# Attention into GELU MLP on one core: how batch 0's masks, transposes and weighing are laid out

## The chip, the cores and the metric

The kernel runs on one core of one Trainium2 chip. The metric is the device time of one launch in microseconds (us), lower is better. The kernel before took 353.18 us (median of 5 runs, 352.17 to 354.53).

## The reference

Eight batches of eight heads, sequence 576, head dimension 64. Each head is causal attention with a forgetting decay; the heads are then joined to tokens of width 512, and the tokens go through a two-layer MLP with exact GELU (width 2048 inside).

```
scores = q @ k.T / sqrt(D)
cum    = cumsum(log(clip(f, 0.0001, 1)))
scores = where(j > i, -1e9, scores + cum[i] - cum[j])
attn   = softmax(scores);  o = attn @ v
x      = o as [B*S, H*D];  h = x @ w_in;  out = gelu(h) @ w_out
```

Inputs and output are float32; the kernel multiplies in bfloat16 and accumulates in float32.

## The kernel before, in words

**Layout.** Heads go in four pairs i = 0 to 3; a pair's q and k lie transposed in `qT[i]`, `kT[i]` as [128, 576], head 0 of the pair on partitions 0 to 63 and head 1 on 64 to 127. Scores are computed transposed (keys on partitions), so the two heads' matmuls of one block contract over 64 rows each, in the two halves of TensorE's array ("64-row tiles"). The causal 576 x 576 square is cut into five key blocks, and these are packed into four score tiles t = 0 to 3 of 448, 448, 448 and 320 columns for each head (`STILES`); tile 0 holds two diagonal blocks, the others one each (`SDIAG`). One score tile takes two PSUM banks (one for each head); the pool `s_psum` has two such tiles, `o_psum` and `m_psum` have two banks each.

**A score tile** (`scores`, L289 to L314): TensorE fills it, ScalarE takes the exponential of all of it into `e` (L314), and the tile is free for the next but one. For batch 0, and for pair 0 of batch 1, the causal mask is added by TensorE ahead of the scores: for each diagonal block and head a 128-row matmul of an identity with `after`, a 128 x 128 tile of 0 and -1e9 (L295), and then the scores on top (L304), cut after the first 128 columns. For all other pairs GpSimd zeroes the masked part of `e` (L316).

**Decay.** The factor exp(-cum[j]) is multiplied into v (and stands beside it as a 65th column) by GpSimd in `weigh_v` (L279, L285), which needs v in `v_sb` and the factors in `wT`; what belongs to the query cancels in the softmax. `attend` (L335) multiplies e with the weighed v for each head into one `o_psum` bank; `normalize` divides by the 65th column on VectorE (L350, L351) and hands the tail of 64 rows on (L361 on VectorE, or L359 on ScalarE for pair 2). `to_xT` transposes the result for the MLP (L373).

**The order of batch 0 is written out by hand** in `first_attention`: warm-up matmuls, the transposes of each pair's k and q (`transposes_first`, L192, copied out by VectorE at L199; pair 0's q by ScalarE), score tiles, the transposition of the factors (L528), `attend_head` for the eight heads between the last two pairs' score tiles, and the first four blocks of the MLP's first product (`gemm1`, L398, GELU at L411). Engines run their own instructions in this order. GpSimd's queue holds, besides, every load of q, k, w_in and w_out (issued by it, and cast on the way): before the attention the masks and the loads of batch 0, and inside it `weigh_v(0, i)`, the quarters of w_in, and q and k of batch 1. SyncE's queue loads v; batch 1's v waits for the memset of `v_sb` that stands behind `weigh_v(0, 3)` on GpSimd.

**After the attention of batch 0** come gemm1 blocks 4 to 15 (`ffb`). Among them stand the transposes of batch 1's pairs 0 to 2 (`transposes_pe`, L220, eight VectorE copies each at L232), after blocks 6, 8 and 13; after block 9 GpSimd is given `weigh_v(1, 0)`, the other quarters of w_out, q and k of batch 2 and `weigh_v(1, 1)`. The transposes of pairs 0 and 1 use `s_psum`, those of pair 2 both banks of `o_psum`. `second_attention` then runs batch 1's scores with the second product of batch 0 (`gemm2`, L438) in the gaps, and transposes pair 3, again into both banks of `o_psum`, after score tile (0, 2). Batches 2 to 7 run in `attention`, with the second product of the batch before in their gaps (L487); the tails of all batches make a last MLP pass.

Of the kernel before, what the change touches and what calls it, by code (L numbers as in the profile page):

```python
# [50 lines left out]
def kernel(  # L51
# [57 lines left out]
    def load_v(b, h0=0, h1=H):  # L109
# [9 lines left out]
    f_sb = consts.tile([BH, S], FP32)  # L119
    nc.sync.dma_start(f_sb, f.rearrange("b h s -> (b h) s"))  # L120
    load_qk_tokens(0, 0, 2)
    ident_bf = consts.tile([P, P], BF16)
    make_identity(nc, ident_bf)
    load_qk_tokens(0, 2, 4)
    load_qk_tokens(0, 4, 6)
    after = consts.tile([P, P], BF16)
    nc.gpsimd.memset(after, 0.0)
    nc.gpsimd.affine_select(
        out=after,
        in_=after,  # L130
        compare_op=Alu.is_ge,
        fill=-1.0e9,
        base=0,
        pattern=[[1, P]],
        channel_multiplier=-1,
    )
    nc.gpsimd.memset(v_sb[:, :, 0, 0:1], 0.0)
    load_v(0, 0, 4)
    load_qk_tokens(0, 6, 8)
# [149 lines left out]
    def scores(b, i, t):  # L289
        on_pe = b == 0 or (b == 1 and i == 0)  # L290
        st = s_psum.tile([P, 2, 512], FP32, tag="s", name=f"s{t}")

        for x, c in enumerate(SDIAG[t] if on_pe else []):
            for h in range(2):
                nc.tensor.matmul(  # L295
                    st[:, h, c : c + P], ident_bf, after, start=x == 0, stop=False
                )
        c, width = 0, sum(w for _, _, w in STILES[t])
        for n, q0, w in STILES[t]:
            cut = P if on_pe and c in SDIAG[t] and w > P else w  # L300
            for a0, a1 in ((0, cut), (cut, w)):
                for h in range(2 if a1 > a0 else 0):
                    d = slice(h * D, (h + 1) * D)
                    nc.tensor.matmul(  # L304
                        st[:, h, c + a0 : c + a1],
                        kT[i][d, K0[n] : K0[n] + P],
                        qT[i][d, q0 + a0 : q0 + a1],
                        start=not on_pe,
                        stop=not on_pe or c + a1 == width,
                    )  # L310
            c += w
        et = e_pool.tile([P, 2, 512], BF16, tag=f"e{t}", name=f"e{t}")
        e_of[b, i, t] = et
        nc.scalar.activation(et[:, :, 0:c], st[:, :, 0:c], Act.Exp, scale=scale)  # L314
        for c0 in [] if on_pe else SDIAG[t]:
            nc.gpsimd.affine_select(  # L316
                out=et[:, :, c0 : c0 + P],
                in_=et[:, :, c0 : c0 + P],
                compare_op=Alu.is_ge,
                fill=0.0,  # L320
                base=0,
                pattern=[[0, 2], [1, P]],
                channel_multiplier=-1,
            )
# [184 lines left out]
    def first_attention():  # L509


        def transposes(i, pool, tag):
            transposes_first(i, 1, pool, tag)
            transposes_first(i, 0, pool, tag)

        def attend_head(i, h):
            attend(0, i, h, (0, 1, 2, 3, 4))
            return normalize(0, i, h)

        warm_up(9)  # L520
        transposes(0, o_psum, "o")
        warm_up(4)
        scores(0, 0, 0)
        transposes(1, m_psum, "m")
        scores(0, 0, 1)
        psw = o_psum.tile([P, NBLK, BH], FP32, tag="o", name="psw")
        for n in range(NBLK):
            nc.tensor.transpose(  # L528
                psw[:, n, :], wk[:, K0[n] : K0[n] + P], ident_fp[:BH, :BH]
            )  # L530
        nc.vector.tensor_copy(wT[:, 0:4, :], psw[:, 0:4, :])
        nc.vector.tensor_copy(wT[D:P, 4, :], psw[D:P, 4, :])
        scores(0, 0, 2)
        scores(0, 0, 3)
        transposes(2, m_psum, "m")
        scores(0, 1, 0)
        scores(0, 1, 1)
        scores(0, 1, 2)
        transposes(3, m_psum, "m")
        scores(0, 1, 3)  # L540
        weigh_v(0, 0)
        load_w_in(0)
        load_w_in(1)
        weigh_v(0, 1)
        load_qk_tokens(1, 0, 4)
        weigh_v(0, 2)
        weigh_v(0, 3)
        load_w_in(2)
        load_w_in(3)
        nc.gpsimd.memset(v_sb[:, :, 0, 0:1], 0.0)  # L550
        load_v(1, 0, 4)
        load_v(1, 4, 8)
        load_qk_tokens(1, 4, 8)
        scores(0, 2, 0)
        attend_head(0, 0)
        scores(0, 2, 1)
        attend_head(0, 1)
        scores(0, 2, 2)
        scores(0, 2, 3)
        attend_head(1, 0)  # L560
        scores(0, 3, 0)
        attend_head(1, 1)
        to_xT(0, 0, nc.vector.tensor_copy)
        scores(0, 3, 1)
        scores(0, 3, 2)
        attend_head(2, 0)
        scores(0, 3, 3)
        attend_head(2, 1)
        to_xT(0, 1, nc.scalar.copy)
        last = [attend_head(3, 0)]  # L570
        both = s_psum.tile([P, 2, 1024], BF16, tag="s", name="ps_x2")
        to_xT(0, 2, nc.scalar.copy, ps=both[:, 0, 0:TC])
        last.append(attend_head(3, 1))

        pss = [gemm1(0, ffb, (0, 1)) for ffb in range(2)]
        to_xT(0, 3, nc.vector.tensor_copy, ps=both[:, 1, 0:TC])
        for tail, r in last:
            nc.vector.tensor_scalar(*tail, r[D:P, 4:5], None, Alu.mult)
        more = s_psum.tile([P, 2, 512], FP32, tag="s", name="ps1")
        pss += [more[:, 0, :], more[:, 1, :]]  # L580
# [88 lines left out]
    for b in range(B):  # L669
# [9 lines left out]
        for ffb in range(0 if b else 4, n_ff):  # L679
            gemm1(b, ffb)  # L680
            if b == 0:
                if ffb in (6, 8, 13):
                    transposes_pe(
                        1, (6, 8, 13).index(ffb), s_psum if ffb < 10 else o_psum
                    )
                if ffb == 9:
                    weigh_v(1, 0)
                    for c in range(1, 4):
                        load_w_out(c)
                    load_qk_tokens(2)  # L690
# [42 lines left out]
```

The softmax here doesn't subtract the row's maximum and nothing guards it: scores larger than these inputs give would overflow.

## Time and profile before

| what | value |
|---|---|
| median of 5 runs | 353.18 us (352.17 to 354.53) |
| the profiled execution | 352.18 us; its span 349.8 us, so 2.4 us lie around the span |
| granted TensorE clock | 0.998 |
| busy: TensorE, ScalarE, VectorE, GpSimd | 338.9, 215.2, 203.6, 124.5 us (97, 62, 58, 36%) |
| warm-up and first transposes (batch 0) | 1.25 to 8.9 us |
| attention of batch 0, up to its first gemm1 matmul | 8.9 to 26.7 us |
| gemm1 of batch 0 | 26.7 to 43.6 us |
| attention of batch 1 with gemm2 of batch 0 | 43.6 to 70.6 us |

Times inside the span are counted from its start. A line of the timeline gives the start, the busy time, the engine, the line of the kernel, the operation with what it writes and reads, the number of instructions merged into it, and in brackets how long the engine was idle before and which engine released it. A line of the chain of waits gives start, length and the work that the end of the program hangs on, merged. TensorE's matmuls are pipelined: the chain shows how long a group holds up what follows, and the timeline's busy time overlaps its neighbours.

### The profile page before, as it was taken

To read this page: it belongs to the slowest core of one execution; us is meant where nothing else is said; L and a number is where in the kernel's file an instruction comes from. 1 tells how busy PE (TensorE), PEld (TensorE's weight loads), DVE (VectorE), ACT (ScalarE), POOL (GpSimd) and SP (SyncE) were. 2 spreads that over 40 slices of the span, in tenths; PEclk is the share of its full clock that TensorE was granted. 3 is DMA by queue.
4 is the path that set the end of the run, shared out by engine and by line. 5 is a ranking of instruction groups with operands and counts; after the bars stand their busy time and mean duration, and the time that the engine had idled before them with its cause. 6 is when DMAs were issued, how large, how long until landed. Compare 5 with 4: busy or idle time off the path is not lost.

```text
span 349.8 us, 7804 instructions
## 1 busy us (share of the span) xinstructions
PE 338.9 (97%) x3122; PEld 176.1 (50%) x3122; DVE 203.6 (58%) x501; ACT 215.2 (62%) x296; POOL 124.5 (36%) x243
## 2 busy tenths in 40 slices
PE   8998989999999999999999999999999999999995
PEld 3674544544555455545554455445544554444443
DVE  4562984596469936894579557956696563011011
ACT  5796586457874787468746874687567774603600
POOL 7390185405538044713453245514450530000000
PEclk9999999999999999999999999999999999999999
DMA  7999999986994999298928893679710131011013
GB/s 109 179 185 188 202 140 177 189 190 134 195 179 127 133 208 155 83 137 165 197 77 123 120 214 104 106 134 209 126 39 0 47 89 41 2 60 60 2 31 89
DMA packets 101219, 43.24 MB, mean 124 GB/s; under 512 B 80000, under 2 KB 96640, under 8 KB 101184
## 3 DMA queue, kind: packets, MB, share of 16 engines
q1 hardware_dynamic: 83888, 28.60, 41.3%
q0 software_dynamic: 16896, 13.63, 26.4%
q8 instruction: 24, 0.39, 0.5%
q10 hardware_dynamic: 400, 0.52, 0.4%
q14 instruction: 11, 0.09, 0.1%
HBM read 36.85 MB, written 9.44 MB: 132 GB/s over the span
## 4 chain that ended last, share of the span: by engine, by line
PE 87%; ACT 9%; issue 2%; DMA 1%; DVE 0%; POOL 0%; ACTq 0%; POOLq 0%
PE ps L398 36%; PE ps L487 18%; PE ps L438 12%; PE o L335 10%; PE s L304 8%; ACT e L314 5%; ACT L314 2%; ACT g L411 2%; PE ps_f L192 1%; PE s L295 1%; DMA k<-in_k_dram 1%; PE ps_x L373 1%; PE ps_w L181 1%; PE ps_t L220 0%; PE s_t L220 0%
## 5 line engine op out<-in xcount | busy, mean ns | idle before, releaser
L411 ACT ACTIVATE g<-ps 128x512 bf16<-128x512 f32 x144 | 85.8, 597 | 83.3 <-PE ps L398 83.3
L314 ACT ACTIVATE e<-s 128x896 bf16<-128x896 f32 (+1 forms) x128 | 103.8, 862 | 30.9 <-PE s L304 30.4
L398 PE MATMUL ps<-xT,w_in_sb 128*128 128x512 bf16 x512 | 112.6, 379 | 1.0 <-ACT g L411 1.0
L487 PE MATMUL ps<-w_out_sb,g 64*128 64x512 bf16 (+1 forms) x690 | 102.3, 376 | 0.0
L316 POOL TENSOR_SCALAR_AFFINE_SELECT e<-e 128x256 bf16<-128x256 bf16 x135 | 53.5, 406 | 113.6 <-ACT e L314 112.4
L398 PEld LDWEIGHTS <-w_in_sb 128*128 128x128 bf16 x576 | 56.0, 98 | 67.9 <-issue 3.0
L279 POOL TENSOR_TENSOR vw<-v_sb,wT 128x640 bf16<-128x640 f32 x32 | 41.1, 1285 | 47.1 <-PE ps L398 15.9
L487 PEld LDWEIGHTS <-g 64*128 64x128 bf16 (+1 forms) x690 | 37.6, 94 | 25.5 <-issue 1.6
L304 PE MATMUL s<-qT,kT 64*128 64x320 bf16 (+5 forms) x424 | 46.8, 272 | 2.5 <-ACT e L314 2.0
L263 DVE COPY qT<-tq 64x288 bf16<-64x288 bf16 x96 | 45.1, 470 | 1.5
L335 PEld LDWEIGHTS <-e 128*128 128x128 bf16 x960 | 35.7, 98 | 17.9 <-issue 11.1
L438 PE MATMUL ps<-w_out_sb,g 128*128 128x512 bf16 (+2 forms) x208 | 44.3, 363 | 0.0
L335 PE MATMUL o<-vw,e 128*128 128x65 bf16 x960 | 41.9, 194 | 0.4 <-ACT e L314 0.4
L495 DVE COPY ot<-ps 128x512 f32<-128x512 f32 x24 | 16.5, 689 | 36.0 <-PE ps L487 36.0
L447 DVE COPY ot<-ps 128x512 f32<-128x512 f32 (+2 forms) x13 | 8.4, 650 | 48.9 <-PE ps L438 48.7
L263 DVE COPY kT<-tk 64x288 bf16<-64x288 bf16 x96 | 32.3, 336 | 1.6
L304 PEld LDWEIGHTS <-kT 64*128 64x128 bf16 x424 | 20.0, 94 | 25.9 <-issue 13.2
L350 DVE RECIPROCAL r<-o 128x5 f32<-128x5 f32 x64 | 12.5, 195 | 29.2 <-PE o L335 28.2
L351 DVE TENSOR_TENSOR x<-o,r 128x256 bf16<-128x256 f32 x64 | 27.2, 425 | 2.2
L438 PEld LDWEIGHTS <-g 128*128 128x128 bf16 x208 | 18.7, 98 | 19.1 <-issue 0.6
L361 DVE TENSOR_SCALAR xt<-o,r 64x64 bf16<-64x64 f32 x60 | 17.4, 290 | 1.4
L497 DVE TENSOR_TENSOR ot<-ot,ps 128x512 f32<-128x512 f32 x24 | 16.5, 687 | 1.3
(61 smaller groups left out, 147.2 us busy)
## 6 DMA issues: line engine op xcount, KB each, us to landing
out_dram<-ot SPq DMA_DIRECT2D x32, 256.0 KB, 2.2
v_sb<-in_v_dram SPq DMA_DIRECT2D x20, 256.0 KB, 4.7
v_sb<-in_v_dram SPq DMA_DIRECT2D x29, 128.0 KB, 5.8
q<-in_q_dram POOLq DMA_DIRECT2D x6, 576.0 KB, 6.5
k<-in_k_dram POOLq DMA_DIRECT2D x6, 576.0 KB, 8.5
w_in_sb<-in_moe_w_in_dram POOLq DMA_DIRECT2D x4, 512.0 KB, 8.2
w_out_sb<-in_moe_w_out_dram POOLq DMA_DIRECT2D x4, 512.0 KB, 8.8
q<-in_q_dram POOLq DMA_DIRECT2D x4, 144.0 KB, 4.6
```

The lines of the kernel that those rows point to most:

```text
L263: nc.vector.tensor_copy(rows[:, odd], src[odd * D : (odd + 1) * D, 2 * i + h].rearrange("d j p -> d p j"),)
L279: nc.gpsimd.tensor_tensor(vw_of[b][:, hs, :, 0:D], v_sb[:, hs, :, :], w.unsqueeze(3).to_broadcast([P, 2, NBLK, D]), Alu.mult,)
L304: nc.tensor.matmul(st[:, h, c + a0 : c + a1], kT[i][d, K0[n] : K0[n] + P], qT[i][d, q0 + a0 : q0 + a1], start=not on_pe, stop=not on_pe or ...
L314: nc.scalar.activation(et[:, :, 0:c], st[:, :, 0:c], Act.Exp, scale=scale)
L316: nc.gpsimd.affine_select(out=et[:, :, c0 : c0 + P], in_=et[:, :, c0 : c0 + P], compare_op=Alu.is_ge, fill=0.0, base=0, pattern=[[0, 2], [ ...
L335: nc.tensor.matmul(o[:, m, :], e_of[b, i, t][:, h, c : c + P], vw_of[b][:, 2 * i + h, n, :], start=(n == 0), stop=(n == m),)
L351: nc.vector.tensor_tensor(x_of[b, i][:, :, h, :], o[:, 0:4, 0:D], r[:, 0:4].unsqueeze(2).to_broadcast([P, NBLK - 1, D]), Alu.mult,)
L361: nc.vector.tensor_scalar(*tail, r[D:P, 4:5], None, Alu.mult)
L398: nc.tensor.matmul(ps, w_in_sb[:, kt, ffb * P : (ffb + 1) * P], src[:, kt, :], start=(kt == 0), stop=(kt == n_dm - 1),)
L411: nc.scalar.activation(g_of[c][ffb], ps, Act.Gelu)
L438: nc.tensor.matmul(pss[ts][:, c0:c1], g_of[c][kt][:, ts * P : (ts + 1) * P], w_out_sb[:, kt, c0:c1], start=(kt == 0), stop=(kt == n_ff - 1),)
L487: nc.tensor.matmul(banks[r], g_of[c][kt][rows, ts * P : (ts + 1) * P], w_out_sb[rows, kt, :], start=(kt == 0), stop=last if r else kt == n ...
```

## The change

- **Masks.** In place of the 128 x 128 `after`, two tiles of [128, 2, 128] are built, `key_of` (ones where partition p is column p + 64·half, an identity in two halves of 64 rows) and `after` (the mask's rows in the same two halves). GpSimd builds both on partitions 0 to 63, and VectorE copies them to 64 to 127. A masked block is now one score matmul over the block's whole width for each head, then two mask matmuls of 64 rows for each head, 64 and 128 columns wide, each head's in the half of the array in which its scores are. This holds wherever TensorE masks: batch 0 and pair 0 of batch 1.
- **Order of batch 0's score tiles.** The transposes of pairs 1 and 2 come one score tile later than before, and later score tiles come ahead of the attends: (0,0) and (0,1) now precede the transposes of pair 1, (1,0) those of pair 2; (0,3) follows the factors' transposition before they are copied out; (2,1) and (2,2) come before head (0,0), (2,3) before (0,1), and so on to (3,3) before head (2,0).
- **GpSimd's queue.** The loads of q and k for pair 1 go ahead of the identity. `weigh_v(0, 0)` to `(0, 3)` stand together, with w_in quarters 0 and 1 after the first two, then the memset of `v_sb` and the loads of batch 1's v; the first half of batch 1's q and k, which stood between `weigh_v(0, 1)` and `(0, 2)`, follows after that, and then w_in quarters 2 and 3.
- **Transposes of batch 1** stand after gemm1 blocks 7, 9 and 15 in place of 6, 8 and 13.

```diff
+    load_qk_tokens(0, 2, 4)
     ident_bf = consts.tile([P, P], BF16)
     make_identity(nc, ident_bf)
-    load_qk_tokens(0, 2, 4)
     load_qk_tokens(0, 4, 6)
-    after = consts.tile([P, P], BF16)
-    nc.gpsimd.memset(after, 0.0)
-    nc.gpsimd.affine_select(
-        out=after,
...
+    key_of = consts.tile([P, 2, P], BF16)
+    after = consts.tile([P, 2, P], BF16)
+    for t, op, fill in (
+        (key_of, Alu.not_equal, 1.0), (after, Alu.is_ge, -1.0e9)
+    ):
+        nc.gpsimd.memset(t[0:D], 0.0)
+        nc.gpsimd.affine_select(
+            out=t[0:D],
+            in_=t[0:D],
+            compare_op=op,
+            fill=fill,
+            base=0,
+            pattern=[[-D, 2], [1, P]],
+            channel_multiplier=-1,
+        )
...
-        for x, c in enumerate(SDIAG[t] if on_pe else []):
-            for h in range(2):
-                nc.tensor.matmul(
-                    st[:, h, c : c + P], ident_bf, after, start=x == 0, stop=False
-                )
-        c, width = 0, sum(w for _, _, w in STILES[t])
+        c = 0
         for n, q0, w in STILES[t]:
-            cut = P if on_pe and c in SDIAG[t] and w > P else w
-            for a0, a1 in ((0, cut), (cut, w)):
-                for h in range(2 if a1 > a0 else 0):
+            masked = on_pe and c in SDIAG[t]
+            for half in range(-1, 2 if masked else 0):
+                for h in range(2):
                     d = slice(h * D, (h + 1) * D)
+                    if half < 0:
+                        to = st[:, h, c : c + w]
+                        ab = kT[i][d, K0[n] : K0[n] + P], qT[i][d, q0 : q0 + w]
+                    else:
+                        last = (half + 1) * D
+                        to = st[:, h, c : c + last]
+                        ab = key_of[d, half, :], after[d, half, 0:last]
                     nc.tensor.matmul(
-                        st[:, h, c + a0 : c + a1],
-                        kT[i][d, K0[n] : K0[n] + P],
-                        qT[i][d, q0 + a0 : q0 + a1],
-                        start=not on_pe,
-                        stop=not on_pe or c + a1 == width,
+                        to, *ab, start=half < 0, stop=half == 1 or not masked
                     )
...
         warm_up(9)
         transposes(0, o_psum, "o")
+        nc.vector.tensor_copy(key_of[D:P], key_of[0:D])
+        nc.vector.tensor_copy(after[D:P], after[0:D])
         warm_up(4)
         scores(0, 0, 0)
+        scores(0, 0, 1)
         transposes(1, m_psum, "m")
-        scores(0, 0, 1)
+        scores(0, 0, 2)
         psw = o_psum.tile([P, NBLK, BH], FP32, tag="o", name="psw")
...
+        scores(0, 0, 3)
         nc.vector.tensor_copy(wT[:, 0:4, :], psw[:, 0:4, :])
         nc.vector.tensor_copy(wT[D:P, 4, :], psw[D:P, 4, :])
-        scores(0, 0, 2)
-        scores(0, 0, 3)
+        scores(0, 1, 0)
         transposes(2, m_psum, "m")
-        scores(0, 1, 0)
         scores(0, 1, 1)
         scores(0, 1, 2)
         transposes(3, m_psum, "m")
         scores(0, 1, 3)
-        weigh_v(0, 0)
-        load_w_in(0)
-        load_w_in(1)
-        weigh_v(0, 1)
-        load_qk_tokens(1, 0, 4)
-        weigh_v(0, 2)
-        weigh_v(0, 3)
-        load_w_in(2)
-        load_w_in(3)
+        for i in range(HP):
+            weigh_v(0, i)
+            if i < 2:
+                load_w_in(i)
         nc.gpsimd.memset(v_sb[:, :, 0, 0:1], 0.0)
         load_v(1, 0, 4)
         load_v(1, 4, 8)
+        load_qk_tokens(1, 0, 4)
+        load_w_in(2)
+        load_w_in(3)
         load_qk_tokens(1, 4, 8)
         scores(0, 2, 0)
+        scores(0, 2, 1)
+        scores(0, 2, 2)
         attend_head(0, 0)
-        scores(0, 2, 1)
+        scores(0, 2, 3)
         attend_head(0, 1)
-        scores(0, 2, 2)
-        scores(0, 2, 3)
+        scores(0, 3, 0)
         attend_head(1, 0)
-        scores(0, 3, 0)
+        scores(0, 3, 1)
         attend_head(1, 1)
+        scores(0, 3, 2)
         to_xT(0, 0, nc.vector.tensor_copy)
-        scores(0, 3, 1)
-        scores(0, 3, 2)
+        scores(0, 3, 3)
         attend_head(2, 0)
-        scores(0, 3, 3)
         attend_head(2, 1)
...
-                if ffb in (6, 8, 13):
+                if ffb in (7, 9, 15):
                     transposes_pe(
-                        1, (6, 8, 13).index(ffb), s_psum if ffb < 10 else o_psum
+                        1, (7, 9, 15).index(ffb), s_psum if ffb < 10 else o_psum
                     )
```

More of the change, by code (lines that the diff above doesn't have):

```diff
@@ L121 @@
     load_qk_tokens(0, 0, 2)
+    load_qk_tokens(0, 2, 4)
     ident_bf = consts.tile([P, P], BF16)
     make_identity(nc, ident_bf)
-    load_qk_tokens(0, 2, 4)
     load_qk_tokens(0, 4, 6)
-    after = consts.tile([P, P], BF16)
-    nc.gpsimd.memset(after, 0.0)
-    nc.gpsimd.affine_select(
-        out=after,
[L130 to L135, printed above, removed]
-    )
+    key_of = consts.tile([P, 2, P], BF16)
[13 more added lines that the diff above has]
+        )
     nc.gpsimd.memset(v_sb[:, :, 0, 0:1], 0.0)
@@ L291, in scores @@
         st = s_psum.tile([P, 2, 512], FP32, tag="s", name=f"s{t}")
-        for x, c in enumerate(SDIAG[t] if on_pe else []):
-            for h in range(2):
-                nc.tensor.matmul(
-                    st[:, h, c : c + P], ident_bf, after, start=x == 0, stop=False
-                )
-        c, width = 0, sum(w for _, _, w in STILES[t])
+        c = 0
         for n, q0, w in STILES[t]:
-            cut = P if on_pe and c in SDIAG[t] and w > P else w
-            for a0, a1 in ((0, cut), (cut, w)):
-                for h in range(2 if a1 > a0 else 0):
+            masked = on_pe and c in SDIAG[t]
+            for half in range(-1, 2 if masked else 0):
+                for h in range(2):
                     d = slice(h * D, (h + 1) * D)
-                    nc.tensor.matmul(
-                        st[:, h, c + a0 : c + a1],
-                        kT[i][d, K0[n] : K0[n] + P],
-                        qT[i][d, q0 + a0 : q0 + a1],
-                        start=not on_pe,
-                        stop=not on_pe or c + a1 == width,
+                    if half < 0:
[5 more added lines that the diff above has]
+                        ab = key_of[d, half, :], after[d, half, 0:last]
+                    nc.tensor.matmul(
+                        to, *ab, start=half < 0, stop=half == 1 or not masked
                     )
```

## The prediction

> **What bounds the kernel now.** I read the page first (TensorE 97% busy, clock 0.998), then the chain of waits, then ScalarE's timeline in batch 0's attention, because all that the change touches lies before 50 us. There the chain changes between TensorE and ScalarE:
>
> ```profile
> 10.79 0.22 PE s L295 x2
> 11.00 0.32 PE s L304 x4
> 11.32 0.02 issue
> 11.34 0.93 ACT e L314
> ...
> 16.74 0.25 PE s L304 x4
> 16.99 0.33 PE s L295 x4
> 17.32 0.30 PE s L304 x8
> 17.62 0.58 PE o L335 x15
> 18.20 0.11 PE s L295 x2
> 18.31 0.30 PE s L304 x4
> ```
>
> The sizes of a switch are in these lines. At 2.4 columns per ns two masks are 256 columns, 0.11; the x4 of L304 stream 448 columns for each head, both heads at once, 0.19. Between attends they take 0.11 + 0.30: 0.11 is lost going into 64-row tiles and out again. Between two masked tiles (16.99) the masks take 0.33 for 0.21: another 0.11 going back to 128 rows.
>
> ```profile
> 11.34 2.34 ACT L314 ACTIVATE e<-s 128x896 bf16<-128x896 f32 x3 [0.60 <-PE s L304]
> 14.24 2.53 ACT L314 ACTIVATE e<-s 128x896 bf16<-128x896 f32 x3 [0.56 <-PE s L304]
> 17.03 4.12 ACT L314 ACTIVATE e<-s 128x640 bf16<-128x640 f32 x5 [0.25 <-PE s L304]
> 21.34 0.92 ACT L314 ACTIVATE e<-s 128x896 bf16<-128x896 f32 x1 [0.18 <-PE s L304]
> 22.55 1.73 ACT L314 ACTIVATE e<-s 128x896 bf16<-128x896 f32 x2 [0.29 <-PE s L304]
> 24.39 0.31 ACT L359 ACTIVATE xt<-o,r 64x64 bf16<-64x64 f32 x1
> 24.72 0.70 ACT L314 ACTIVATE e<-s 128x640 bf16<-128x640 f32 x1
> ```
>
> ScalarE starves for TensorE five times in these lines, 1.9 us in all. Where it doesn't (11.34 to 12.17, 14.24 to 15.06) exponentials of 896 start 0.82 apart, one of 640 is passed in 0.63. Sixteen need 12 x 0.82 + 4 x 0.63 = 12.4 us, and take 9.83 to 25.42. The last is late since an `xt` stands before it in the queue.
>
> Later, at the seam of batches 0 and 1, VectorE and ScalarE matter:
>
> ```profile
> 44.21 1.28 ACT L314 ACT_TABLE_LOAD   x1
> 44.72 1.95 DVE L232 COPY kT<-ps_t 64x288 bf16<-64x288 bf16 x4
> 46.47 0.27 PE L295 MATMUL s<-after,ident_bf 128*128 128x128 bf16 x2 [0.90 <-ACT e L314]
> 47.44 1.95 DVE L232 COPY qT<-ps_t 64x288 bf16<-64x288 bf16 x4 [0.77 <-PE ps_t L220]
> ```
>
> VectorE copies batch 1's transposes back to back, 3.96 us for each pair (34.80, 38.76, 42.72), and is done 0.77 before it gets pair 3's. DMA is nearly full:
>
> ```profile
> 20.00:30.00 10.00, 9.22 (x152) 6.16 (x149) 5.84 (x19) 8.47 (x14) 6.83 (x11) 1.00 1.25 197
> 30.00:40.00 10.00, 9.37 (x63) 4.83 (x63) 5.05 (x11) 5.73 (x11) 0.00 (x0) 1.00 1.24 193
> ```
>
> The last two columns are the DMA share and GB/s: the engines are full from 18 to 43 us.
>
> **What the Trainium skill says.** "TensorE: Matmul & The Clock Gate", "The mechanism": matmuls in different row groups run at once; the 0.30 of the x4 above agrees (one after another would be 0.37 without a switch). The same page, "Back-to-back issue gap", puts a floor of about 25 ns under a small matmul: that is my upper price for a pair of 64-wide masks, 2 x 25 = 50 ns; the lower is their 64 columns, 27 ns; no such pair is in the trace as a mask. "ScalarE: Activation LUTs", "What ACT_TABLE_LOAD costs": back-to-back activations overlap by some 93 ns; here 0.92 long and 0.82 apart. "DMA: Bandwidth & Descriptors", "Issuing engines are not separate DMA queues": v from SyncE and weights from GpSimd share the same engines, as the full DMA rows above let one expect.
>
> **The change, part by part.**
>
> *Masks.* Before, a pair has five blocks x 2 x 128 columns = 0.53 us of masks. After: five x (64 + 128) columns, both heads at once, 0.40; with 50 ns for the narrow pair 0.52. A tile's columns become 832, 640, 640, 512, that is 0.35, 0.27, 0.27, 0.21 us, plus 0.11 where a 128-row group is the neighbour. Gain 0 to 0.13 for each pair; I take 0.1. Masks also stop switching: where score tiles follow one another nothing is lost.
>
> *Building the masks.* Two memsets and two selects over 256 columns instead of one each over 128. A 128-wide memset and select take 0.30 and 0.24 from start to next start (5.96, 6.26, 6.50); with twice the columns some 0.42 and 0.36, so 1.56 for 0.54: the memset of v, batch 0's v loads and pair 3's q, k are issued 1.0 later. Pair 3's q, k land at 12.9 behind a full queue and are needed after 14. v paces `weigh_v(0,0)`, at 14.70; its loads took 5.4 to 6.1 us in a full queue, so part of the 1.0 is absorbed: I take 0.3, bounds 0 and 1.0. Its reader, head (0,0), comes at 17.4 against 16.5: hidden, and still with 0.9. The identity, behind two loads more (0.65 each), is ready at 4.8; the first transposes wait for k until 5.67. VectorE's two copies (some 0.2 each) run at 7.4 to 7.8; masks are first wanted at 9. All nothing, covered by the loads and the warm-up.
>
> *Order.* I went through TensorE's and ScalarE's queues with these durations: an exponential starts when ScalarE is free (0.82 or 0.63) and its tile is filled; a tile is filled when TensorE gets there and the exponential two before has ended (start + 0.92 or 0.70, + 0.04). Transposes 0.74, attend 0.58. Up to 10.2 us TensorE streams at half rate (warm-up matmuls 0.43 apart), so tile (0,0) ends at 9.7.
>
> ```
> exponential of   (0,1)  (1,0)  (1,1)  (1,3)  (2,0)  (2,3)  (3,0)  (3,1)  (3,3)
> before           11.34  14.24  15.06  17.03  17.66  20.46  21.34  22.55  24.72
> after, worked    10.54  12.82  13.93  15.57  16.20  18.66  19.40  20.40  22.20
> ```
>
> 0.8 comes from (0,1) ahead of pair 1's transposes, 0.6 more from (1,0) ahead of pair 2's. Pair 3's q transposes then wait 0.2 for VectorE's copy of pair 2's q (`m_psum`), under an exponential. (3,3) no longer stands behind an `xt`. Head (3,0), which got its last input at 25.48, runs at 23.2 to 23.8; head (3,1) ends at 24.65. The chain's first L398 began at 26.67: 2.0 earlier. What is late next is each small refill by TensorE (0.1 to 0.2 at (3,0), (3,1), (3,2)), counted.
>
> *GpSimd's queue.* `weigh_v` ends at 16.5, 18.5, 20.7, 22.0 (1.28 + 0.22, and 0.79 for each load between); heads want them at 17.4, 19.3, 21.8, 23.2: the smallest gap 0.8. The DMA order stays the same. q, k of batch 1 are issued 3.2 later, at 22.2, but the quarter of w_in ahead of them lands only at 25.3 + 0.3. Batch 1's v is issued 2.5 earlier and takes its share (0.045 of 0.2 MB per us after 28 us) earlier, so what stands behind lands some 0.6 later, less once v is done. w_in's third quarter landed at 31.1 and would at 31.9; block 8 wants it at 33.6. The fourth: 35.3 for 37.6. Pair 2's k: 39.3 for 40.7. w_out's first: 42.0 before, 42.9 after, wanted at 41.8: 1.1 of waiting, under the pause for the table load and the exponential (next score at 44.0) and the next point. All hidden.
>
> *Transposes after blocks 7, 9, 15.* The third set (0.51) no longer stands ahead of block 14's GELU, so the last GELU, the table load and batch 1's first exponential come 0.5 earlier still. But VectorE starts 0.86 later (four matmuls of 0.215) and its chain of copies ends 0.86 later against TensorE: pair 3's k transposes, which need pair 2's second bank, wait until 45.55 and end at 45.8, instead of 47.66 with no wait. So of 2.0 + 0.5, 1.85 arrives there; the pair 0 masks of batch 1 behind give 0.05.
>
> *Sum.* 1.9 us. From 50 us on TensorE is 100% busy in the windows and all its weights come earlier, so the gain should stay. Profiled 352.18 - 1.9 = 350.3; the median of runs stands 1.0 above that execution, so 353.18 - 1.9 = 351.3.
>
> **Rivals.**
> - *The refill holds it.* If each of the twelve large tiles waits out the end of the one before (0.93 apart, as in the chain, not 0.82), 12 x 0.11 = 1.3 is lost, of which the refills already counted (0.4) are part: gain 1.0, 352.2. For: `s_psum` has two tiles only. Against: 0.82 is seen where TensorE was ahead.
> - *Given back to DMA.* The seam pays for w_out or block 8 for w_in: about 1 us, 352.4. For: full DMA rows. Against: gaps of 1.3 to 2.3 us by my landings.
> - *Slower.* One place: block 8 waiting for w_in's third quarter, if the q, k loads issued at 22.2 leave the queue empty, or v's earlier stream takes half of it. Each us of landing past 33.6 costs one; past 35.5 (31.1 before) the kernel is slower; at 36.6 it gives 354.3. For: issue leads the queue's end by only 3.4 us. Against: w_in's first quarter, issued at 16.06, moved at the full rate from 18.
> - *Seam without the wait.* If VectorE's copies hold nothing, 2.5 arrive: 350.7.
> - That the masks are no cheaper costs 0.4 and belongs to the forecast's spread.
>
> **Chances.** Forecast 0.59 (own range 350.6 to 352.0), refill 0.13, DMA 0.12, slower 0.10, no wait 0.06. The range reaches from 350.3 to 353.3. 0.5% (1.8 us) is about what a measurement can tell from no change; the forecast lies just past it, so I give two thirds of its chance to faster: with the last case 0.47; same 0.43, slower 0.10.
>
> **What would show it.** Right: ScalarE's pauses between the first and last exponential of batch 0 under 0.8 us in all (1.9 in the lines above); the first gemm1 matmul near 24.6; no mask group of 128 rows; a wait of TensorE's pair 3 transposes for VectorE near 45; score tile (0,3) of batch 1 near 47. Wrong: exponentials 0.9 apart, a wait at gemm1 block 8 or at the first gemm2 matmuls longer than the pause there, or `weigh_v(0,0)` after 16.

## The result, and the profile after

| | before | after |
|---|---|---|
| median | 352.89 us (351.50 to 356.71, 80 runs) | 355.41 us (351.84 to 358.73, 43 runs) |
| ratio to before | | 1.0041, 95% interval 1.0025 to 1.0056 |
| the profiled execution, span, granted clock | 352.18, 349.8, 0.998 | 356.37, 354.1, 0.990 |

The change makes the kernel slower: 0.4% by the ratio, 2.5 us by the medians. The ratio leaves out executions over 1.5% above the fastest of the same kernel (7 of the 44 of after), the medians keep them. Forecast were 351.3 us and a range of 350.3 to 353.3, so both the size and the sign are wrong.

The chain of waits on the page of after, in shares of the span:

```profile
PE 76%; DMA 8%; ACT 7%; POOL 3%; SPq 3%; issue 1%; DVE 0%; POOLq 0%; ACTq 0%
PE ps L401 31%; PE ps L490 18%; PE ps L441 12%; PE o L338 8%; PE s L311 6%; ACT e L317 4%; DMA w_out_sb<-in_moe_w_out_dram 4%; DMA v_sb<-in_v_dram 4%; SPq L114 3%; ACT L317 2%; POOL vw L285 1%; ACT g L414 1%; PE ps_x L376 1%; POOL q L102 1%; POOL k L102 1%
```

Before, TensorE had 87% of it and DMA 1%. Now w_out has 4%, and v with the queue that issues it 7%: that is the first thing to see, ahead of any timeline.

**The attention of batch 0 did get faster.** ScalarE's timeline of the kernel after, where `e` are exponentials and `g` GELUs:

```profile
8.22 4.08 ACT L317 ACTIVATE e<-s 128x896 bf16<-128x896 f32 x5 [0.84 <-PE s L311]
12.51 1.73 ACT L317 ACTIVATE e<-s 128x896 bf16<-128x896 f32 x2 [0.21 <-PE s L311]
14.60 3.73 ACT L317 ACTIVATE e<-s 128x640 bf16<-128x640 f32 x5 [0.36 <-PE s L311]
18.65 0.92 ACT L317 ACTIVATE e<-s 128x896 bf16<-128x896 f32 x1 [0.32 <-PE s L311]
19.87 2.47 ACT L317 ACTIVATE e<-s 128x896 bf16<-128x896 f32 x3 [0.30 <-PE s L311]
...
26.85 1.57 ACT L414 ACTIVATE g<-ps 128x512 bf16<-128x512 f32 x3 [0.78 <-PE ps L401]
...
42.29 1.28 ACT L317 ACT_TABLE_LOAD   x1 [0.43 <-PE s L311]
```

Before, the first GELU stands here:

```profile
29.01 1.57 ACT L411 ACTIVATE g<-ps 128x512 bf16<-128x512 f32 x3 [0.84 <-PE ps L398]
```

ScalarE's waits for scores between the first and the last exponential sum to 1.2 us (1.9 before), and the first GELU starts at 26.85 for 29.01. So 2.16 us are gained in this pair of executions, and at the table load of the seam (ScalarE fetches the table of exponentials again) 1.9 are still there (42.29 for 44.21).

**They are lost twice, both times to w_out.** TensorE's timeline of the kernel after (scores are L311, gemm2 L441):

```profile
42.23 0.25 PE L311 MATMUL s<-after,key_of 64*128 64x64 bf16 x4
44.52 1.04 PE L441 MATMUL ps<-w_out_sb,g 128*128 128x512 bf16 x4 [2.04 <-ACT e L317]
...
48.60 0.37 PE L311 MATMUL s<-qT,kT 64*128 64x320 bf16 x4 [0.67 <-ACT e L317]
...
48.91 0.36 PE L338 MATMUL o<-vw,e 128*128 128x65 bf16 x6
52.47 1.01 PE L441 MATMUL ps<-w_out_sb,g 128*128 128x512 bf16 x2 [3.20 <-DMA w_out_sb<-in_moe_w_out_dram]
53.41 0.56 PE L311 MATMUL s<-qT,kT 64*128 64x448 bf16 x2
...
54.39 1.47 PE L441 MATMUL ps<-w_out_sb,g 128*128 128x512 bf16 x3
```

The same places before:

```profile
44.53 1.04 PE L438 MATMUL ps<-w_out_sb,g 128*128 128x512 bf16 x4
...
49.73 0.37 PE L304 MATMUL s<-qT,kT 64*128 64x320 bf16 x4 [0.66 <-ACT e L314]
...
50.23 0.59 PE L438 MATMUL ps<-w_out_sb,g 128*128 128x512 bf16 x2
```

The first wait of after is put down to `e`, but gemm2 doesn't read `e`: it reads g and w_out, and w_out's first quarter, issued at 26.66, landed 17.8 later, at 44.5. Before, the same group started at 44.53 without a wait, so the lead is used up at this point; it comes back in part (the scores behind `e` start at 48.60 for 49.73), since the score tiles ahead of it were early. The second wait is plain: 3.20 us for w_out's second quarter. Before, that group began at 50.23 without one.

Then the clock. The same kernel by stretches (columns: busy time and instructions of TensorE, its weight loads, VectorE, ScalarE, GpSimd; then granted clock, DMA share, GB/s):

```profile
20.00:30.00 10.00, 8.53 (x121) 5.29 (x118) 5.07 (x17) 7.31 (x12) 7.35 (x12) 1.00 1.23 198
30.00:40.00 10.00, 9.84 (x66) 4.97 (x65) 6.28 (x14) 5.98 (x11) 3.17 (x5) 1.00 1.24 194
...
48.00:50.00 2.00, 0.66 (x10) 0.38 (x10) 1.93 (x5) 2.00 (x3) 0.56 (x2) 1.00 1.21 109
50.00:52.00 2.00, 0.00 (x0) 0.00 (x0) 0.27 (x1) 0.17 (x1) 0.69 (x2) 0.61 0.91 107
52.00:54.00 2.00, 1.53 (x6) 0.31 (x6) 0.00 (x0) 0.00 (x0) 1.29 (x3) 0.50 1.27 202
54.00:56.00 2.00, 2.00 (x14) 0.78 (x14) 0.91 (x3) 0.92 (x1) 0.95 (x2) 0.50 1.29 206
56.00:58.00 2.00, 2.00 (x24) 1.17 (x22) 0.72 (x3) 0.70 (x1) 1.28 (x3) 0.69 1.31 203
```

From 20 to 40 DMA is as full as before. TensorE stood still from 49.3 to 52.5; its clock falls to half at 50.4, in the middle of this wait, and stays there until 57.2: three matmuls of L441 take 1.47 above, 0.81 at full clock (e1 at 52.39). The books of the two profiled executions, by how much after is ahead (-) or behind (+): -2.16 at the first GELU, -1.13 behind w_out's first quarter, +2.24 at the second, +4.3 when batch 1's attention is over, and +4.3 at the end (354.1 for 349.8). So in this pair of executions 1.0 goes to the first quarter, 3.4 to the second and 2.1, the rest, to the clock.

**Why w_out is late.** The DMA rows in slices of half a microsecond from 36 to 56, first of before, then of after:

```profile
DMA  9999999999996976500669999999999999999999
GB/s 192 196 195 195 193 198 203 195 217 270 267 230 126 225 180 132 82 9 0 53 37 162 207 180 205 186 156 201 211 199 176 182 137 160 203 186 216 200 201 201
...
w_out_sb<-in_moe_w_out_dram POOLq DMA_DIRECT2D x3, 512.0 KB, 7.6
...
tails<-xt SPq DMA_TRANSPOSE x1, 3.1
```

```profile
GB/s 193 192 192 197 188 190 192 193 203 188 196 198 196 193 206 196 219 188 194 190 193 171 157 137 116 112 107 101 69 34 123 201 204 199 198 205 210 203 201 211
...
w_out_sb<-in_moe_w_out_dram POOLq DMA_DIRECT2D x3, 512.0 KB, 15.6
...
tails<-xt SPq DMA_TRANSPOSE x1, 16.2
```

What GpSimd and SyncE issued, first of before, then of after:

```profile
42.51 1.99 SPq L385 DMA_TRANSPOSE tails<-xt  x1
...
42.78 1.28 POOL L279 TENSOR_TENSOR vw<-v_sb,wT 128x640 bf16<-128x640 f32 x1 [15.94 <-PE ps L398]
...
44.14 2.31 POOL L159 DMA_DIRECT2D w_out_sb<-in_moe_w_out_dram  x3
```

```profile
36.83 1.28 POOL L285 TENSOR_TENSOR vw<-v_sb,wT 128x640 bf16<-128x640 f32 x1 [9.38 <-DMA v_sb<-in_v_dram]
...
36.89 5.58 SPq L388 DMA_TRANSPOSE tails<-xt  x1
...
38.20 2.31 POOL L165 DMA_DIRECT2D w_out_sb<-in_moe_w_out_dram  x3
```

Before, the queues run dry at 45, and the tails' DMA transpose (`x_tail_dma`, SyncE, issued at 42.5) lands in 3.1 us. After, there is no lull: GpSimd got batch 1's v at 36.83 rather than 42.78, so three quarters of w_out and batch 2's q, k are issued 6 us earlier. The transpose, issued at 36.9, lands 16.2 later, and from 46.5 the rate sinks step by step to 34 GB/s, until 51. The packet records of after show what sinks (q0 is GpSimd's queue, q1 SyncE's; start of the half microsecond from the span's start, packets started in it, kB, median and longest packet in ns):

```
 45.50 q0 n=  74 kB=  75.8 med=  96 max=  129 | q1 n=  77 kB=  19.2 max=   82
 46.00 q0 n=  80 kB=  76.8 med=  96 max= 4761 | q1 n=  78 kB=  19.7 max=   31
 47.00 q0 n=  65 kB=  62.5 med=  96 max= 3719 | q1 n=  66 kB=  15.9 max= 3729
 50.00 q0 n=  28 kB=  26.6 med=  96 max= 1116 | q1 n=  32 kB=   7.9 max= 1202
 51.50 q0 n=  85 kB=  86.0 med=  96 max=  153 | q1 n=  81 kB=  14.7 max=  102
```

Single packets of both queues last 4.8, 3.7, 1.2 us, the later they start the shorter: 27 of them start between 46.4 and 50.8, and all end at 51.2 to 51.3. It looks as if each DMA engine that comes to its part of the transpose stands still, with both queues, until the last one comes to it. That picture is inferred; that the transpose is what does it is tested below.

### The profile page after: what moved, and what is told of

It is laid out like the page before. It is cut to its first block, busy times and chain, and to the rows that moved or that the text cites. A ratio compares the mean times of both kernels' runs of the same rounds, so it can differ in the third digit from the quotient of the medians.

```text
span 354.1 us, 7830 instructions
## 1 busy us (share of the span) xinstructions
PE 337.2 (95%) x3132; PEld 175.3 (50%) x3132; DVE 204.0 (58%) x503; ACT 215.0 (61%) x296; POOL 125.6 (35%) x245
## 4 chain that ended last, share of the span: by engine, by line
PE 76%; DMA 8%; ACT 7%; POOL 3%; SPq 3%; issue 1%; DVE 0%; POOLq 0%; ACTq 0%
PE ps L401 31%; PE ps L490 18%; PE ps L441 12%; PE o L338 8%; PE s L311 6%; ACT e L317 4%; DMA w_out_sb<-in_moe_w_out_dram 4%; DMA v_sb<-in_v_dram 4%; SPq L114 3%; ACT L317 2%; POOL vw L285 1%; ACT g L414 1%; PE ps_x L376 1%; POOL q L102 1%; POOL k L102 1%
## 5 line engine op out<-in xcount | busy, mean ns | idle before, releaser
L311 PE MATMUL s<-qT,kT 64*128 64x320 bf16 (+4 forms) x384 | 47.2, 283 | 3.7 <-ACT e L317 3.2
L441 PE MATMUL ps<-w_out_sb,g 128*128 128x512 bf16 (+2 forms) x208 | 45.5, 369 | 5.2 <-DMA w_out_sb<-in_moe_w_out_dram 3.2
L269 DVE COPY qT<-tq 64x288 bf16<-64x288 bf16 x96 | 43.4, 452 | 1.5
L269 DVE COPY kT<-tk 64x288 bf16<-64x288 bf16 x96 | 33.9, 353 | 1.6
L311 PEld LDWEIGHTS <-kT 64*128 64x128 bf16 x384 | 20.2, 94 | 28.1 <-issue 16.2
L441 PEld LDWEIGHTS <-g 128*128 128x128 bf16 x208 | 19.0, 99 | 24.6 <-issue 4.1
```

Source lines behind the costliest of these rows:

```text
L269: nc.vector.tensor_copy(rows[:, odd], src[odd * D : (odd + 1) * D, 2 * i + h].rearrange("d j p -> d p j"),)
L311: nc.tensor.matmul(to, *ab, start=half < 0, stop=half == 1 or not masked)
L441: nc.tensor.matmul(pss[ts][:, c0:c1], g_of[c][kt][:, ts * P : (ts + 1) * P], w_out_sb[:, kt, c0:c1], start=(kt == 0), stop=(kt == n_ff - 1),)
```

## The experiments

Each kernel of the table has 14 to 64 executions to a set; e7 and e8, with one each, are left out of it. The executions fall into two groups by mean granted clock, 0.998 and above or 0.995 and below. The table gives the share of executions with a dropped clock, and the median span of either group. It doesn't say where the clock dropped: in the traces of after, e1, e3 and e6 that is in batch 1's attention, from 47 us on, in those of e4, e9 and e12 it is in batch 0's attention.

| kernel | median us | ratio to before (95%) | clock dropped | span, full clock | span, dropped |
|---|---|---|---|---|---|
| before (four sets) | 353.0 to 353.5 | | 42 of 174 | 350.5 to 350.9 | 352.5 to 352.9 |
| after | 355.41 | 1.0041 (1.0025 to 1.0056) | 40 of 44 | 350.4 | 353.4 |
| e1 transpose late | 352.85 | 0.9984 (0.9960 to 1.0008) | 7 of 14 | 349.6 | 350.7 |
| e2 old GpSimd queue | 353.14 | 1.0017 (0.9996 to 1.0039) | 7 of 22 | 350.3 | 352.4 |
| e3 old places of transposes | 355.40 | 1.0059 (1.0036 to 1.0082) | 15 of 19 | 351.1 | 353.4 |
| e4 before, new queue only | 353.33 | 1.0023 (1.0001 to 1.0045) | 8 of 22 | 350.6 | 354.2 |
| e5 after, loads by need | 351.17 | 0.9938 (0.9917 to 0.9959) | 3 of 14 | 348.8 | 349.7 |
| e6 before, loads by need | 354.46 | 1.0038 (1.0019 to 1.0056) | 9 of 22 | 351.7 | 353.6 |
| e9 e1 + w_out's second early | 352.92 | 0.9991 (0.9968 to 1.0013) | 12 of 22 | 349.9 | 351.1 |
| e10 e5, transpose early | 356.04 | 1.0062 (1.0037 to 1.0088) | 19 of 22 | 351.1 | 354.2 |
| e11 before, transpose late | 353.23 | 0.9998 (0.9973 to 1.0023) | 4 of 14 | 350.2 | 352.6 |
| e12 e5, old masks | 350.82 | 0.9940 (0.9918 to 0.9961) | 2 of 19 | 348.6 | 350.4 |

### The transpose: e1, and the other half of it, e11

```diff
             load_w_out(0)
-            x_tail_dma(0)
...
         load_v(2, 4, 8)
+        x_tail_dma(0)
```

> The changed kernel with one line moved: the DMA transpose of batch 0's tails (needed only in the last MLP pass) is issued at the end of batch 1's attention, not ahead of gemm1 block 4. Theory 'the transpose stops the DMA engines': in the changed kernel it stands in SyncE's rings behind batch 1's v, in a full queue, and the engines stop one by one from 46.5 until all have reached it at 51.3; w_out's second quarter lands at 52.4 and TensorE waits 3.2 us and falls to half clock. Without it no packet takes over 1 us there, that quarter lands near 48.5, and the time is 351.0 to 352.3 us, 3 to 4 below the changed kernel and about 1 below the kernel before. Rival 'the queue is just too full' (w_out, q, k and v compete for the same bytes per us, the transpose only shares): the quarter still lands after 51 and the time stays within 1 us of the changed kernel's 355.4.

352.85, 0.55 above the range of my theory. The stall is gone (no packet of either queue over 0.2 us from 44 to 54, 184 to 219 GB/s in all slices from 36 to 56), and so is the wait for the second quarter. TensorE's waits of e1, 20 to 80 us:

```profile
PE ps L441 <- DMA w_out_sb<-in_moe_w_out_dram: 2.0, 1, 2.0
PE ps L401 <- ACT g L414: 1.0, 1, 1.0
```

What is left is the first quarter, landing at 45.3 and costing 2.0; half of the executions have a clock drop. So the transpose's place accounts for some 2.5 us of the medians, and another cause keeps the rest of the gain. The same edit on the kernel before:

> The kernel before with only the tails' DMA transpose moved to the end of batch 1's attention. Theory: before, the transpose met an empty queue and landed in 3 us; nothing waited for it, so the time is that of before within 0.2%: 352.3 to 353.5. Rival, the transpose late is a gain in any kernel: 350.5 to 351.5.

353.23, ratio 0.9998, as the theory has it: before, the transpose cost nothing.

### Undoing the parts: e2, e3, e4

e2 is after with the GpSimd queue of before in batch 0.

> The changed kernel with GpSimd's queue in batch 0 as before (q, k of batch 1 and two quarters of w_in between the weighings, v's memset after them); masks, score order and transposes after blocks 7, 9, 15 stay. Theory: the loss comes from batch 1's v starting 2.5 us earlier, so that its weighing no longer holds w_out's other quarters back until the queue is empty (36.8 instead of 42.8). With the old order the weighing ends near 42 again, the pause of DMA returns and the gain of the attention shows: 351.0 to 352.0 us. Rival 'order or masks or the later transposes cost at the seam': the time stays at 354 to 356.

353.14, above the theory's range and below the rival's. Two waits of TensorE in e2, 8 to 80 us, tell why:

```profile
PE ps L441 <- DMA w_out_sb<-in_moe_w_out_dram: 1.8, 2, 1.5
...
PE o L338 <- POOL vw L291: 0.7, 1, 0.7
```

With the loads between the weighings, the heads wait for `vw`, and the first GELU comes at 28.27, only 0.7 ahead of before; and even this late queue leaves w_out's second quarter 1.5 behind. The gain in the attention needs the new queue, and the new queue brings the trouble in DMA.

e3 is after with batch 1's transposes back behind blocks 6, 8 and 13.

> The changed kernel with batch 1's transposes after gemm1 blocks 6, 8, 13 as before. Theory: DMA decides at the seam, TensorE and VectorE have slack there while w_out is waited for, so nothing moves: 354.5 to 356. Rival 'the later transposes are what costs at the seam': 352 to 353.

355.40, as the theory has it: their places don't matter in after.

e4 is the kernel before with only the new GpSimd queue.

> The kernel before with only GpSimd's queue in batch 0 changed (weighings together, batch 1's v earlier, q and k later). Theory: the same crowd at the seam without the gain in the attention: batch 1's weighing leaves before 40, the tails' transpose falls into a full queue, w_out's second quarter lands after 50.4, where TensorE wants it: 354 to 357 us, slower than the kernel before by 1 to 4. Rival 'the queue is innocent': within 0.5 us of the kernel before, 352.4 to 353.4.

353.33: below the theory's range and inside the rival's. The DMA row of e4 from 36 to 56 shows the same stall, deeper than in after:

```profile
GB/s 188 193 191 193 189 194 191 197 193 197 197 211 184 199 254 237 197 203 202 195 152 64 62 54 49 51 48 34 33 11 13 154 196 185 207 207 223 191 208 204
```

But w_out's second quarter is used only at 53.13 in that execution (its clock was down from 11.4 to 21.7, and TensorE was late), and nobody waits for it. In this trace the stall does no harm, as TensorE isn't early enough to want what it holds. That may be why the new queue is near harmless with the old order and isn't with the new one; of e4's executions at full clock (14 of 22, 0.1 us above before) no trace was kept.

### Loads in the order of need: e5, e6

e5 is after with four moves of loads and weighings; `x_tail_dma(0)` goes to the end of batch 1's attention as in e1, and `load_v` takes the issuing engine as an argument.

```diff
             load_w_out(0)
-            x_tail_dma(0)
+            load_w_out(1)
...
         load_v(1, 0, 4)
-        load_v(1, 4, 8)
...
-                    for c in range(1, 4):
+                    for c in range(2, 4):
                         load_w_out(c)
+                    load_v(1, 4, 8, nc.gpsimd)
...
-                if i == 1 and t in (0, 2):
+                if i == 2 and t in (0, 2):
                     weigh_v(1, 2 + t // 2)
```

> The changed kernel with batch 1's loads ordered by when they are wanted: w_out's second quarter directly behind its first; the second half of batch 1's v not on SyncE's queue but behind w_out's fourth quarter on GpSimd's, its two weighings one pair later; the tails' transpose at the end of batch 1's attention. Theory 'the seam is bound by DMA: what the attention gains is waited away for w_out': now w_out's first quarter lands near 43 (44.5 in the changed kernel) and its second near 46 (52.4), TensorE waits under 0.7 us for both together, and the 2 us of the attention arrive: 350.6 to 351.6 us, 1.4 to 2.3 below the kernel before. Rival 'the gain is lost elsewhere too': 352.3 to 353.3, as with the transpose moved alone.

351.17, ratio 0.9938: inside the theory's range, and 2 us below the kernel before. TensorE's gemm2 groups of e5:

```profile
42.40 1.04 PE L441 MATMUL ps<-w_out_sb,g 128*128 128x512 bf16 x3
45.88 1.03 PE L441 MATMUL ps<-w_out_sb,g 128*128 128x512 bf16 x4
48.60 0.59 PE L441 MATMUL ps<-w_out_sb,g 128*128 128x512 bf16 x2
```

None waits for DMA (the first quarter landed at 42.4), and the third starts 1.6 before that of the kernel before (50.23). A gain of the forecast's size, 1.9 us, is there once the loads allow it: at full clock the span is 348.8 against 350.9 in the same set.

> The kernel before with the same reordering of loads, and nothing of the change. Theory: there w_out's first quarter lands 2.5 us and its second 0.7 us ahead of TensorE, so earlier loads gain nothing: 352.5 to 353.3. Rival 'the reordering is the gain': under 352.

354.46, slower than before and outside the range. In e6 batch 1's v comes as late as before, and GpSimd then has more to issue in front of its work. Its timeline:

```profile
45.42 1.27 POOL L279 TENSOR_TENSOR vw<-v_sb,wT 128x640 bf16<-128x640 f32 x1 [17.04 <-DMA v_sb<-in_v_dram]
...
48.31 3.64 POOL L114 DMA_DIRECT2D v_sb<-in_v_dram  x5
...
53.77 1.29 POOL L279 TENSOR_TENSOR vw<-v_sb,wT 128x640 bf16<-128x640 f32 x1
54.99 0.23 POOL L285 CAST vw<-wT 128x10 bf16<-128x10 f32 x1
55.14 2.55 POOL L316 TENSOR_SCALAR_AFFINE_SELECT e<-e 128x256 bf16<-128x256 bf16 x7
```

Five v loads hold GpSimd for 3.64 us, and the masks of `e` start at 55.14 (before at 50.57). TensorE waits 1.4 us for them. By itself the load order costs 1 us; with the earlier attention it is what lets the gain through.

### Which of e5's moves counts: e9, e10

e9 is e1 with w_out's second quarter right behind the first, and v left on SyncE.

> The kernel after, with the tails' DMA transpose at the end of batch 1's attention and w_out's second quarter issued right behind the first; batch 1's v stays whole on SyncE's queue. Theory: the stall of the DMA engines and the wait at w_out's second quarter are gone, the wait at its first (1 to 2 us, because v and q,k still share the queue) stays and costs some clock: 351.5 to 352.5. Rival, the order of v alone makes the difference between 352.85 and 351.17: no better than the kernel with only the transpose late, 352.6 to 353.1. Second rival, w_out's first quarter is not late enough to matter: 351.0 to 351.4.

352.92: the theory misses, the first rival holds. An early second quarter adds nothing to e1, whose second quarter was in time already. In e9 the first quarter is used at 45.60 after a wait of 0.75, though the profiled TensorE was some 2.5 us late (its clock was down from 15.8 to 22.7, in the attention of batch 0); in e5 it landed at 42.4. The two kernels differ only in the second half of v and its weighings, so moving that half is what brings w_out forward: by the packet records SyncE's queue moves nothing from 36.5 to 55 us in e5, and some 0.02 MB in each half microsecond from 33 to 46 in e9.

e10 is e5 with one line back in its old place: `x_tail_dma(0)` behind `load_w_out(1)`, ahead of gemm1 block 4.

> The fastest kernel so far (351.17: w_out's second quarter early, half of batch 1's v behind the last quarter) but with the tails' DMA transpose where the kernel after has it. Theory: what stalls the DMA engines is the transpose behind the second half of v, which here comes later, so little is left of the stall before w_out's second quarter; a short stall may hold w_out's last quarters or q,k of batch 2: 351.2 to 352.2. Rival, the transpose in any full queue stops the engines for some 5 us: a hole in the DMA rate below 120 GB/s near 38 to 46 us and 352.5 to 354.5.

356.04, the slowest of all, and 4.9 us above e5. The rival's cause holds (the time is above even its range), and my theory that the second half of v is needed for the stall falls. The DMA row of e10 from 34 to 44, in quarters of a microsecond:

```profile
GB/s 207 196 195 206 183 196 166 98 101 81 58 61 41 25 25 16 12 11 135 203 181 204 198 200 209 198 223 200 195 200 208 197 205 214 209 201 209 209 197 221
```

From 35.5 to 38.5 the rate sinks to 11 GB/s; the transpose, issued at 27.1, lands 13.3 later. Now w_in is late: gemm1 waits 1.34 for it until 39.7 (a wait of 0.56 ends at 34.3, ahead of the stall, which doesn't explain it). This pair is the cleanest test of the transpose. At full clock e10 is 2.3 us above e5 (351.1, 3 executions, and 348.8); the rest goes with the clock, which dropped in 19 of 22 executions. The profiled one kept it, so where it drops is not seen.

### The masks: e7, e8, e12

e7 is before with the 64-row masks alone, e8 is after with the old masks; both are single executions.

> The kernel before with the 64-row masks alone. Worked price: 0.1 us for each pair and 0.1 for each switch saved, of which part is under ScalarE: the first gemm1 matmul 0.4 to 1.0 us earlier than in the kernel before. If a 64-row mask were dearer than priced, not earlier at all.

353.07; the first GELU is at 29.26 (before 29.01). `weigh_v(0, 0)` started at 15.99 for 14.70. The gain expected isn't seen.

> The changed kernel with the masks of before (128-row identity). Worked price: 1.0 to 1.6 us of the attention's gain come from the order alone, so the first gemm1 matmul is that much earlier than in the kernel before; the wait at w_out's second quarter stays over 1 us.

353.88; the first GELU is at 27.46 (after 26.85). By this pair order and queue give 1.5 of the 2.2 us. But in e1 and e3, whose code up to there is that of after, the first GELU comes at 27.57 and 27.41, so the pair shows no difference. e12 is e5 with the old masks.

> The fastest kernel (351.17; loads in the order of need) with the masks of the kernel before, 128 rows and both heads in one matmul group, in place of the 64-row ones. Theory: the masks were worth some 0.1 us for each pair and 0.1 to 0.2 for switches between them, 0.6 us in batch 0 together, and nothing later takes it back: 351.6 to 352.0, the first GELU at 27.4 to 27.7 in an execution without a clock drop. Rival, they are worth nothing since ScalarE paces the attention either way: 351.0 to 351.4.

350.82, 0.9940, against 0.9938 for e5; at full clock 348.6 and 348.8. The loss of 0.6 us that my theory expects isn't seen: cheaper masks are worth nothing that these measurements can tell. Each ratio is known to 0.2%, or 0.75 us, so that a few tenths of a microsecond are not ruled out. The order, the queue and the loads give e12 its 2 us without the new masks. e5 and e12 beat both kernels, and no difference between them is shown.

## Why the prediction was wrong, point by point

What failed is the part behind the attention: w_out's first quarter was held to be hidden and all later weights to come earlier, so that DMA at the seam was priced at nothing.

- *Order and queue: right in the main.* Worked out were 2.0 us up to the first gemm1 matmul; the profile has 2.15 (24.36 for 26.51), but e1 and e3, with the same code up to there, gain 1.4 and 1.6. That it is near 2 in the profile is in part luck of the execution: the second group of four warm-up matmuls took 1.89 before and 1.04 after, as TensorE was still at half rate before, and the first exponential came at 8.22 for 9.83. That start is not the whole gain: e6, with the old order, queue and masks, also took 1.04 there, started its exponentials at 8.26 and had its first GELU only at 28.83. e2 (new order, old queue, 28.27) says that the order needs the queue; no run has the order alone. The pauses of ScalarE, forecast under 0.8, are 1.2. The last exponential began by 21.7, worked out 22.2.
- *Masks: not shown.* 0 to 0.13 for each pair, 0.1 taken; e12 sees no gain. (The masks and the switches were priced on TensorE; this stage also hangs on ScalarE and the weighing.)
- *Building the masks: mostly hidden.* `weigh_v(0, 0)` moved from 14.70 to 15.10 (worked 15.0). Pair 3's k, held to land in time, came 0.6 late: TensorE waited for it at 13.4.
- *GpSimd's queue: the step that failed.* "w_out's first: 42.0 before, 42.9 after, wanted at 41.8: 1.1 of waiting ... All hidden." It landed at 44.5. I priced batch 1's v at 0.045 MB per us, its rate in the full queue after 28 us. By the packet records it moved 0.27 MB from 24 to 28 (0.07 per us), and 1.00 MB by the time that GpSimd's queue had delivered w_out's first quarter (before 0.78); that queue had also started 0.1 MB late. Some 0.32 MB at its 0.15 MB per us are 2.1 us by this estimate, for 2.5 measured (44.5 - 42.0). The two queues take turns by packets: 74 packets of 1024 bytes against 77 of 256 in the first half microsecond of the packet records above, as the Trainium skill states ("DMA: Bandwidth & Descriptors", "Queues, rings and completion order").
- *"All its weights come earlier": the step that cost most.* I followed v's earlier landing to GpSimd's work and no further. It is also what releases three w_out quarters and q, k of batch 2, 6 us earlier, so the lull at 45 that the tails' transpose used disappears. I hadn't listed that transpose at all: it is one line in SyncE's queue behind v, and it moved from 42.5 to 36.9. Cost: 3.4 us in the profiled execution. That the transpose's place is the cause e1 and e10 show, with 2.5 and 4.9 us of the medians, clock included.
- *The clock: not in the forecast.* I added waits as if they only cost their length. The Trainium skill ("TensorE: Matmul & The Clock Gate", "What's actually happening") says that TensorE falls to half clock after an idle window of some 3.4 us, and that the windows run free of the kernel. The length agrees: by the clock records the half-clock stretches inside the kept traces last 3.41 (e1, e3, e6, e12), 6.83 (after, e9) and 10.24 us (e4), and mean clocks cluster near 0.995, 0.990 and 0.985 to match. The condition doesn't agree. No wait of TensorE here lasts 3.4 us; in the 3.41 us ahead of the drop TensorE was busy for 1.59 us in after, 1.60 in e1, 1.45 in e3 and 1.89 in e6, while e2 kept its clock after such a stretch with 1.88. So waits of 1.4 in all (e6) to 3.2 us can drop the clock and need not. After, 40 of 44 executions have a drop, of before 42 of 174. What a drop costs varies: half its length on paper, 1.7 us for one stretch, where TensorE is never idle; but executions of before with one stretch have a median span 1.6 above those at full clock, those with three (16 executions) only 2.0. How much of the medians' difference is the clock isn't shown. At full clock after is 350.4 (4 executions) and before 350.5 to 350.9, but the profiled execution was 2.2 behind before it lost anything to the clock, so these four seem to have had shorter waits too.
- *Transposes behind blocks 7, 9, 15.* The wait of 0.4 for VectorE is seen in e2, which is early enough to meet it; after itself shows none, as it waits for w_out first. e3 says that the places don't matter here.
- *The rivals.* "Given back to DMA" had the place (the seam pays for w_out) but a quarter of the price (1 us for 1.0 and 3.4). "Slower" needed w_in's third quarter, which wasn't late in after; e10 shows that such waits can come, the longer of its two from the transpose. In the chances, two thirds of 0.59 and 0.06 make 0.45, not 0.47; nothing hangs on it.

Still open: how the transpose stops the engines, since every run tests only its place; what exactly drops the clock, and where e10's other executions drop theirs; and whether the masks are worth a few tenths.

## What to carry to other kernels

When an edit lets work start earlier, list everything that is issued behind it on that queue, DMA transposes too, and look up whether the trace of before gave each of them an empty queue. Give a wait of TensorE of about 2 us a chance of a half-clock stretch of 3.4 us behind it; here the executions with one stretch lie some 1 us (e5) to 3 us (e4) above those at full clock, part of which can be their longer waits. Take cheaper TensorE work next to a busy ScalarE as nothing until a run shows otherwise (here none did). Order the loads by when they are needed before shortening a stage in front of them.

## What the runs showed of the hardware

- The tails' DMA transpose landed in 3.1 us in a draining queue, and in 13.3 to 16.2 us in a full one. The long landing is that of its neighbours (loads of v beside it took 16.0 and 16.4); what sets it apart is that the rate of both queues sank to 34 GB/s (after) and 11 GB/s (e4, e10) for some 3 to 5 us, with packets of up to 4.8 and 5.4 us that all ended together. The Trainium skill ("Advanced Engine Details and Errata", "X-Bar Transpose (TRN2)") calls transpose DMAs as fast as regular ones; the landing in the full queue fits that. That a transpose can hold up both queues, as here, the page doesn't say, and no regular load did so in e1 (44 to 54 us) or e5 (30 to 54).
- Two queues that took turns by packets shared the bytes by packet size: v, in 256-byte packets, got a fifth of the bytes beside w_out's 1024-byte ones, though half of the packets (74 of one and 77 of the other in half a microsecond of after).
- TensorE's clock went to half for whole multiples of 3.41 us, also in the middle of a wait, and after stretches in which TensorE was still busy for 43 to 66% of the time. Executions of one kernel differ, among other things, by the number of such stretches and by where they fall: after ranges from 351.84 to 358.73 us.
